# A layer norm turned by VectorE through exchanged reads, and two shifts in a hand-written order

## The chip, the cores and the metric

The kernel runs on one core of a Trainium2 chip. The metric is the device time of one launch in microseconds (us). Beside the matrix engine (PE) the core has VectorE (DVE), ScalarE (ACT) and GpSimd (POOL); SyncE (SP) issues nearly all DMAs, in order, and waits there for whatever a transfer needs.

## What is computed

One transformer block over 2,048 tokens of 1,024 channels: layer norm, linear attention with a learned feature map, output projection and residual; then layer norm, an MLP with relu over 3,584 channels, and residual. All in float32.

```python
def _layernorm(x, axis=-1, eps=1e-5):
    m = jnp.mean(x, axis=axis, keepdims=True)
    v = jnp.var(x, axis=axis, keepdims=True)
    return (x - m) / jnp.sqrt(v + eps)
...
        qkv = (lambda x, *d: x.transpose(*d))((x @ wqkv).reshape(B, S, 3, H, Dh), 2, 0, 3, 1, 4)
        q, k, v = qkv[0], qkv[1], qkv[2]
        pq = jnp.einsum("bhsd,hdf->bhsf", q, w_phi)
        pk = jnp.einsum("bhsd,hdf->bhsf", k, w_phi)
        phi_q = jnp.concatenate([_softmax(pq, axis=-1), _softmax(-pq, axis=-1)], axis=-1)
        phi_k = jnp.concatenate([_softmax(pk, axis=-1), _softmax(-pk, axis=-1)], axis=-1)
        kv = jnp.einsum("bhsf,bhsd->bhfd", phi_k, v)
        z  = jnp.einsum("bhsf->bhf", phi_k)
        num = jnp.einsum("bhqf,bhfd->bhqd", phi_q, kv)
        den = jnp.einsum("bhqf,bhf->bhq", phi_q, z)[..., None] + 1e-6
        o = num / den
        return (lambda x, *d: x.transpose(*d))(o, 0, 2, 1, 3).reshape(B, S, D) @ wo
...
    def _B_ref(x, w1, w2):
        h = jnp.einsum("bsd,df->bsf", x, w1)
        zero = jnp.zeros_like(h)
        h = jnp.maximum(h, zero)
        return jnp.einsum("bsf,fd->bsd", h, w2)
...
    x = A_x
    h = x + _A_ref(_layernorm(x, axis=-1), A_wqkv, A_w_phi, A_wo)
    h2 = h + _B_ref(_layernorm(h, axis=-1), B_w1, B_w2)
```

## The kernel before

**Products.** Every float32 product is made of three matmuls of a rounded type (L182, L183, L184): high half by high half, and the two mixed ones. So each weight tile of 128x512 comes in as `raw` (SP), is rounded to its high half by ACT (L125), and its low half, `raw` less the high one, is made by POOL or by DVE (L129). A ring of such weights lies ahead of PE; the engines work their queues in order. The activations are split in the same way.

**Stages and steps.** The program is written as one list of pieces of work. PE's part is counted in *steps*, one step being one set of three matmuls of 128x512; `when(step, f)` puts a piece of work of another engine, or a small product, beside that step. Eight steps make an item up to step 1,024, four after that. Steps 0 to 255 make keys and values of the first half of the tokens, 256 to 383 the queries of that half in two slabs of 64 steps (the second from 320), 384 to 767 the same for the second half, 768 to 1,023 the output projection with the rest of the attention beside it, then come the up products (from 1,024) and the down products of the MLP.

**Weight sums.** The MLP is done by Strassen and Winograd's scheme: seven products of half-size blocks instead of eight. Sums of weight blocks are made beforehand on POOL, 56 groups of them: `t_load` (SP, 512 KB, L352), four subtractions of 128x256 `t_sum` (POOL, L362) and `t_store` (SP, L365), at the steps of the table `sums_at` (L1090). The groups of the first half's query slabs use two buffers in turn. POOL's low halves (L129) stand in the same queue.

**The second layer norm.** The 16 token tiles are taken in pairs, `i` = 0 to 3 in each of the two halves ("near", b=0, done beside the output projection, and "late" or "far", b=1, beside the up products). `ln_pair` (L692) has stages: load of the two tiles from `hd` (SP), statistics (DVE, L221), scale (POOL, L230 to L232), the norm (ACT, L238, 128x1024 each), turning by PE in four groups of four transposes of 128x128 (`ln_turn`, L245; and L714) with copies out of PSUM (ACT, L247), the sums that the scheme needs of the tokens (DVE, L718 and L719; POOL, L724 and L725), and seven stores to `hs` (`ln_store`, L728). The table `LN2` (L1051) gives the steps of the stages: near pairs from 832 in distances of 40, far pairs from 1,084 in distances of 68. `h_load` (L738) later brings the turned tiles from `hs` into `hT` in 128x4x128 pieces; ACT (L750) and DVE (L754) split them for the up products. The first half's `hT` loads fall around step 1,024, when `hd` stores of the residual (L687) leave too.

**PSUM.** The up products go round four banks `mm` and two others (`ac`, `tp`); ACT (L777) or DVE (L780) drains a bank, and PE may write it again only then.

## Time and profile before

| | |
|---|---|
| time, median of 3 runs | 1894.32 us (1893.66 to 1894.36) |
| the profiled execution | 1895.65 us, its span 1893.9 us |
| granted PE clock, mean | 0.998 |
| PE | 1879.6 us busy, 11,640 matmuls |
| DVE, ACT, POOL | 1048.3, 740.3, 975.9 us busy |
| DMA | 432.17 MB, mean 228 GB/s |

The span runs from the first to the last instruction of the profiled execution. Busy time of PE is modelled, since its matmuls are pipelined: one is shown with 0.39 us while the next starts 0.23 us after it. So PE is best read from the starts of its matmuls, and a place where it stood still from the brackets of the timeline and the view of waits. The other engines may idle without cost as long as what they make is there in time.

### The profile page before, as it was taken

Reading aid. Unit: us, or ns where it says so; the run is one execution under the profiler, and the core shown is the slowest. Engines: PE = TensorE matmul, PEld = TensorE weight load, DVE = VectorE, ACT = ScalarE, POOL = GpSimd, SP = SyncE. Lnnn points to the kernel's source line nnn. Section 1 sums busy time; section 2 is a strip of 40 time slices with the busy share of each in tenths; the row PEclk is TensorE's granted clock in tenths of the full one; section 3 lists DMA queues with packets and bytes.
Section 4 is the critical chain, followed back from the end, with each engine's and each line's share of the span. In section 5 each row is a group of like instructions: output and inputs, shape, how many; then the busy total and the mean of one; then the engine's idle time right before and its main releaser. Section 6 shows DMA issues by size and latency. Waiting matters only on the chain.

```text
span 1893.9 us, 31847 instructions
## 1 busy us (share of the span) xinstructions
PE 1879.6 (99%) x11640; PEld 1541.0 (81%) x11640; DVE 1048.3 (55%) x1687; ACT 740.3 (39%) x1258; POOL 975.9 (52%) x959
## 2 busy tenths in 40 slices
PE   9999999999999999999999999999999999999999
PEld 7777778888788787888888888888888888888887
DVE  6787668677689776555544563334333433343333
ACT  5322235222233122255454554444444444444442
POOL 4887743888936988323333222222344444444443
PEclk9999999999999999999999999999999999999999
DMA  7888687566555676796877986666677677767775
GB/s 224 289 292 290 228 284 253 187 197 199 186 195 175 205 243 211 251 271 212 276 229 244 296 271 218 184 194 204 216 238 218 197 233 237 240 212 219 215 215 179
DMA packets 292365, 432.17 MB, mean 228 GB/s; under 512 B 24048, under 2 KB 150000, under 8 KB 292208
## 3 DMA queue, kind: packets, MB, share of 16 engines
q1 hardware_dynamic: 275312, 413.36, 68.8%
q10 hardware_dynamic: 16896, 16.78, 2.6%
q8 instruction: 91, 1.49, 0.3%
q14 instruction: 66, 0.54, 0.1%
HBM read 292.68 MB, written 137.36 MB: 227 GB/s over the span
## 4 chain that ended last, share of the span: by engine, by line
PE 87%; POOL 7%; DMA 3%; issue 1%; DVE 1%; SPq 0%; ACT 0%; POOLq 0%; ACTq 0%
PE mm L182 22%; PE mm L183 22%; PE mm L184 22%; PE ac L182 4%; PE ac L184 4%; PE ac L183 4%; PE tp L182 2%; PE tp L184 2%; PE tp L183 2%; POOL ez L575 2%; POOL b L362 1%; PE tp L245 1%; DMA b<-in_w_dram 1%; POOL w L129 1%; POOL qe L613 1%
## 5 line engine op out<-in xcount | busy, mean ns | idle before, releaser
L129 POOL TENSOR_TENSOR w<-raw,w 128x512 fp32r<-128x512 f32 x353 | 468.2, 1328 | 733.1 <-ACT w L125 696.4
L125 ACT ACTIVATE w<-raw 128x512 fp32r<-128x512 f32 x686 | 409.6, 628 | 506.1 <-PE mm L184 249.9
L129 DVE TENSOR_TENSOR w<-raw,w 128x512 fp32r<-128x512 f32 x333 | 272.1, 818 | 525.2 <-ACT w L125 522.0
L182 PE MATMUL mm<-w,xT 128*128 128x512 f32 x768 | 306.4, 399 | 0.0
L183 PE MATMUL mm<-w,xT 128*128 128x512 f32 x768 | 301.5, 393 | 4.1 <-POOL w L129 3.8
L184 PE MATMUL mm<-w,xT 128*128 128x512 f32 x768 | 300.4, 391 | 0.0
L182 PE MATMUL mm<-hT,w 128*128 128x512 f32 x672 | 262.6, 391 | 0.0
L183 PE MATMUL mm<-hT,w 128*128 128x512 f32 x672 | 261.7, 389 | 0.5 <-DVE hT L754 0.5
L184 PE MATMUL mm<-hT,w 128*128 128x512 f32 x672 | 261.6, 389 | 0.0
L183 PEld LDWEIGHTS mm<-w,xT 128*128 128x128 f32 x768 | 144.9, 189 | 34.6 <-POOL w L129 5.6
L362 POOL TENSOR_TENSOR b<-b 128x256 f32<-128x256 f32 x176 | 144.6, 822 | 54.9 <-DMA b<-in_w_dram 44.7
L182 PEld LDWEIGHTS mm<-w,xT 128*128 128x128 f32 x768 | 144.9, 189 | 34.2 <-issue 2.9
L184 PEld LDWEIGHTS mm<-w,xT 128*128 128x128 f32 x768 | 144.9, 189 | 30.9
L182 PE MATMUL mm<-w 128*128 128x512 f32 x392 | 152.5, 389 | 0.0
L183 PE MATMUL mm<-w 128*128 128x512 f32 x392 | 152.5, 389 | 0.0
L184 PE MATMUL mm<-w 128*128 128x512 f32 x392 | 152.5, 389 | 0.0
L183 PEld LDWEIGHTS mm<-hT,w 128*128 128x128 f32 x672 | 126.2, 188 | 26.8 <-DVE hT L754 1.1
L184 PEld LDWEIGHTS mm<-hT,w 128*128 128x128 f32 x672 | 126.2, 188 | 26.3
L182 PEld LDWEIGHTS mm<-hT,w 128*128 128x128 f32 x672 | 126.2, 188 | 25.8
L182 PEld LDWEIGHTS mm<-w 128*128 128x128 f32 x392 | 73.6, 188 | 15.3
L184 PEld LDWEIGHTS mm<-w 128*128 128x128 f32 x392 | 73.6, 188 | 15.3
L183 PEld LDWEIGHTS mm<-w 128*128 128x128 f32 x392 | 73.6, 188 | 15.2
(170 smaller groups left out, 3143.9 us busy)
## 6 DMA issues: line engine op xcount, KB each, us to landing
raw<-t SPq DMA_DIRECT2D x224, 256.0 KB, 3.8
raw<-ad SPq DMA_DIRECT2D x196, 256.0 KB, 3.0
raw<-in_w_dram SPq DMA_DIRECT2D x168, 256.0 KB, 3.0
ad<-c SPq DMA_DIRECT2D x112, 256.0 KB, 3.5
b<-in_w_dram SPq DMA_DIRECT2D x44, 512.0 KB, 5.7
t<-b SPq DMA_DIRECT2D x44, 512.0 KB, 5.0
ad<-s SPq DMA_DIRECT2D x84, 256.0 KB, 4.1
ed<-qe ACTq DMA_DIRECT2D x32, 512.0 KB, 4.3
```

What stands on the lines that cost most here:

```text
L125: nc.scalar.activation(w[:, 0, :], raw[1], AF.Copy)
L129: eng.tensor_tensor(out=w[:, 1, :], in0=raw[1], in1=w[:, 0, :].bitcast(F32), op=ALU.subtract)
L182: pe.matmul(ps, a_hi, b_hi, start=first, stop=False, skip_group_check=more)
L183: pe.matmul(ps, a_hi, b_lo, start=False, stop=False, skip_group_check=more)
L184: pe.matmul(ps, a_lo, b_hi, start=False, stop=last, skip_group_check=more)
L245: pe.transpose(pt[:, k, :], xn[:, (4 * j + k) * P:(4 * j + k + 1) * P], ident)
L362: pool.tensor_tensor(out=tsum[*u, *out], in0=tsum[*u, *a], in1=tsum[*u, *b], op=ALU.subtract)
L575: pool.tensor_tensor(out=ez, in0=e_q[u].rearrange("p (i h) s f -> p i (h s f)", i=4)[:, 2 * j:2 * j + 2, :], in1=zb[:, q, None, 256 * r:25 ...
L613: pool.tensor_tensor(out=e, in0=e, in1=sd[:, :, None].to_broadcast([P, 32, 32]), op=ALU.mult)
```

## The change

Three things are changed.

1. *Far pairs.* PE no longer turns them. The statistics of a far tile are taken by DVE from the residual sum while it is in the core (`far_stats`), POOL makes the scale as before, and `far_scale` writes mean and scale of each token, repeated four times, to a small DRAM tensor `scd` in pieces of 8 bytes. `far_pair` then loads the tile with *exchanged reads*: four DMAs of 32 partitions, so that a partition holds pieces of 128 channels of eight tokens; a reload of `scd` brings the scales into the same places. ACT norms it in eight pieces of 128x256 of one pair, in one stage; DVE turns each 32x32 block (`far_swap`), which with the exchange gives the turned tile. The sums follow as before. The stores and `h_load` for b=1 have other patterns: 512 pieces of 512 bytes a store; four DMAs of 32x4x256 for what were two of 128x4x128.
2. *Weight sums.* In the first half's query slabs six and four groups (9 and 12 steps apart) become four and five (10 apart), and one group moves to step 650.
3. *Near pairs 1 and 2.* The turn of pair 1 comes six steps later (its stores four); the loads of pair 2 come six steps later and the stages after that are drawn together.

```diff
+    scd = [dram.tile([2, 4 * P * 2], F32, name=f"scd{i}") for i in range(4)]
...
+    def far_stats(t, hf):
+        if hf == 0:
+            hst[t] = hp.tile([P, 2, 6], F32, name="hst", bufs=8)
+        v.bn_stats(out=hst[t][:, hf, :], in_=xh[t, hf])
+        if hf == 1:
+            xst["h", t] = mv = lnp.tile([P, 2], F32, name="mv", bufs=4)
+            v.bn_aggr(out=mv, in_=hst.pop(t))
+
+    def far_scale(t):
+        dst = scd[t % 4][t % HT // 4].rearrange("(a p s) -> p a s", a=4, s=2)
+        sp.dma_start(dst, xst.pop(("h", t))[:, None, :].to_broadcast([P, 4, 2]))
+
+    def far_swap(dst, src):
+        v.transpose(dst.rearrange("p (c t g) -> p g c t", c=8, g=4), src.rearrange("p (g c k) -> p g c k", g=4, c=8))
+
+    def far_pair(i, stage):
+
+        tiles = [HT + 4 * r + i for r in range(2)]
+        if stage < 2:
+            t = tiles[stage]
+            xnt["h", t] = x = lnp.tile([P, D], F32, name="xin")
+            for a in range(4):
+                sp.dma_start(x[32 * a:32 * (a + 1)].rearrange("t (g r f) -> t g r f", g=4, r=2),
+                             hd[t].rearrange("(t g) (r a f) -> a t g r f", g=4, r=2, a=4)[a])
+        elif stage == 2:
+            sp.dma_start(scx[:, 2 * i:2 * i + 2].rearrange("p r g s -> p r (g s)"),
+                         scd[i].rearrange("r (p f) -> p r f", f=8))
+        elif stage == 3:
+            for r, t in enumerate(tiles):
+                for g in range(4):
+                    x, sc = xnt["h", t][:, 256 * g:256 * (g + 1)], scx[:, 2 * i + r, g]
+                    act.activation(x, x, AF.Identity, bias=sc[:, 1:2], scale=sc[:, 0:1])
+        elif stage == 4:
+            x1, x2 = (xnt.pop(("h", t)) for t in tiles)
+            y2 = mp.tile([P, D], F32, name="y2", bufs=1)
+            sums[1, i] = x1, x2, y2
+            far_swap(y2, x2)
+        elif stage == 5:
+            s, y1, y2 = sums[1, i]
+            far_swap(y1, s)
...
+        sp.dma_start(hs[1, m][:, :, i], t.rearrange("p (k n) -> p k n", k=4))
...
+        if b == 0:
+            lo = hT[m][:, 1, :, cols].rearrange("p k (i n) -> p k i n", i=2)
+            for i in range(2):
+                sp.dma_start(f32(lo[:, :, i, :]), hs[b, m][:, 2 * g + i])
+            return
+        src = hs[b, m].rearrange("(a k) q i n -> q k a (i n)", a=4)
+        for q in range(4):
+            sp.dma_start(f32(hT[m][32 * q:32 * (q + 1), 1, :, cols]), src[q, :, :, cols])
...
+        if t >= HT:
+            when(added, far_stats, t, hf)
+            if hf == 1:
+                when(added + 4, ln_power, ("h", t))
+                when(added + 15, far_scale, t)
...
-    LN2 = ((0, 9, 12, 17, 24, 25, 26, 27, 29, 36), (0, 18, 26, 32, 40, 42, 44, 46, 50, 60))
+    NEAR = {1: (0, 9, 12, 17, 30, 31, 32, 33, 35, 40), 2: (6, 14, 17, 20, 24, 25, 26, 27, 29, 36)}
+    FAR = 0, 4, 8, 28, 34, 38, 42, 46, 54
...
-    sums_at = [30, 39, 47, 55] + [64 * i + k for i in (1, 2, 3, 4) for k in sixth] + [332, 344, 356, 368] + \
-        [64 * i + k for i in (6, 7, 8, 9) for k in sixth]
+    sums_at = [30, 39, 47, 55] + [64 * i + k for i in (1, 2, 3) for k in sixth] + \
+        [266, 276, 286, 296, 332, 342, 352, 362, 372] + [64 * i + k for i in (6, 7, 8, 9) for k in sixth] + [650]
```

What this does to the order of three queues follows; the changed kernel's lines are numbered a little higher (L362 becomes L363, L777 L843, L742 L804).

POOL, around the first half's query slabs (`b` are the weight sums, `w` the low halves of weights). Before:

```order
L362 TENSOR_TENSOR b<-b 128x256 x2
L129 TENSOR_TENSOR w<-raw,w 128x512
L362 TENSOR_TENSOR b<-b 128x256 x21
L129 TENSOR_TENSOR w<-raw,w 128x512
L362 TENSOR_TENSOR b<-b 128x256
L129 TENSOR_TENSOR w<-raw,w 128x512 x4
L362 TENSOR_TENSOR b<-b 128x256 x16
L129 TENSOR_TENSOR w<-raw,w 128x512 x4
```

Now:

```order
L363 TENSOR_TENSOR b<-b 128x256 x2
L129 TENSOR_TENSOR w<-raw,w 128x512
L363 TENSOR_TENSOR b<-b 128x256 x14
L129 TENSOR_TENSOR w<-raw,w 128x512 x5
L363 TENSOR_TENSOR b<-b 128x256 x20
L129 TENSOR_TENSOR w<-raw,w 128x512 x4
```

Before, 23 subtractions stand ahead of the first low half of the second slab and one more ahead of the next four; now 16 in all, and 20 instead of 16 ahead of the four after them.

ACT, in the up products where the third far pair is normed (`c<-mm` drains a PSUM bank, `w<-raw` is a high half). Before:

```order
L777 ACTIVATE c_10889<-mm 128x512
L125 ACTIVATE w<-raw 128x512
L777 ACTIVATE c_10926<-mm 128x512
L125 ACTIVATE w<-raw 128x512
L238 ACTIVATE xin<-xin,sc 128x1024 x2
L777 ACTIVATE c_10959<-mm 128x512
```

Now:

```order
L843 ACTIVATE c_10917<-mm 128x512
L125 ACTIVATE w<-raw 128x512
L769 ACTIVATE xin<-xin,scx 128x256 x8
L843 ACTIVATE c_10954<-mm 128x512
L125 ACTIVATE w<-raw 128x512
L843 ACTIVATE c_10985<-mm 128x512
```

The norms stood behind the second of these drains; the eight new ones stand ahead of it.

SP, around the start of the up products (`hd<-xh` stores the residual sum, `raw` loads weights, `hT<-hs` loads the turned tiles, `scd` are the new little writes). Now:

```order
L688 DMA hd_97<-xh 128x512
L748 DMA scd_114<-sc 128x4x2
L804 DMA hT_9207<-hs_2_103 128x4x128 x2
L338 DMA raw<-in_w_dram 128x512
L688 DMA hd_98<-xh 128x512
L338 DMA raw<-in_w_dram 128x512
L748 DMA scd_115<-sc 128x4x2
L688 DMA hd_99<-xh 128x512
L338 DMA raw<-t_2_316 128x512
L338 DMA raw<-t_3_317 128x512
L748 DMA scd_116<-sc 128x4x2
L804 DMA hT_9637<-hs_7_104 128x4x128 x2
```

The same rows stood there without the three `scd` writes; a fourth one follows two `hT` loads later, and four stand earlier, beside the stores of the first four far tiles.

More of the change, by code (lines that the diff above doesn't have):

```diff
@@ L687, in wo_store, with ln_pair @@
         sp.dma_start(hd[t][:, hf * 512:(hf + 1) * 512], xh.pop((t, hf)))
-    def ln_pair(b, i, stage):
-        keys = [("h", HT * b + 4 * r + i) for r in range(2)]
+    def ln_pair(i, stage):
+        keys = [("h", 4 * r + i) for r in range(2)]
         if stage == 0:
@@ L723, in ln_pair @@
-            s4 = (mp or hp).tile([P, 512], F32, name="s4l", bufs=1)
+            x1, s12 = xnt[keys[0]], sums[0, i]
+            s4 = hp.tile([P, 512], F32, name="s4l", bufs=1)
             pool.tensor_tensor(out=s12[:, 1, :], in0=s12[:, 0, :], in1=x1[:, 0:512], op=ALU.subtract)
             pool.tensor_tensor(out=s4, in0=x1[:, 512:], in1=s12[:, 1, :], op=ALU.subtract)
-            sums[b, i] = s12, s4
-    def ln_store(b, i, j):
-        x1, x2 = (xnt["h", HT * b + 4 * r + i] for r in range(2))
-        s12, s4 = sums[b, i]
+            sums[0, i] = s12, s4
@@ new lines @@
+    hst = {}
+    def far_scale(t):
[27 more added lines that the diff above has]
+            far_swap(y1, s)
+        elif stage == 6:
+            s, y1, y2 = sums[1, i]
+            v.tensor_add(s[:, 0:512], y2[:, 0:512], y2[:, 512:])
+            v.tensor_sub(y2[:, 0:512], y1[:, 0:512], y2[:, 0:512])
+        elif stage == 7:
+            s, y1, y2 = sums[1, i]
+            s4 = mp.tile([P, 512], F32, name="s4l", bufs=1)
+            pool.tensor_tensor(out=s[:, 512:], in0=s[:, 0:512], in1=y1[:, 0:512], op=ALU.subtract)
+            pool.tensor_tensor(out=s4, in0=y1[:, 512:], in1=s[:, 512:], op=ALU.subtract)
+            sums[1, i] = s, y1, y2, s4
@@ L1054 @@
     for i in range(4):
+        near, far = wo0 + 64 + 40 * i, up0 + 60 + 68 * i
+        ln2 = NEAR.get(i, (0, 9, 12, 17, 24, 25, 26, 27, 29, 36))
         for stage in range(9):
-            when(wo0 + 64 + 40 * i + LN2[0][stage], ln_pair, 0, i, stage)
-            when(up0 + 60 + 68 * i + LN2[1][stage], ln_pair, 1, i, stage)
+            when(near + ln2[stage], ln_pair, i, stage)
+        for stage in range(8):
+            when(far + FAR[stage], far_pair, i, stage)
         for j in range(7):
-            when(wo0 + 64 + 40 * i + LN2[0][9] + j // 2, ln_store, 0, i, j)
-            when(up0 + 60 + 68 * i + LN2[1][9] + j, ln_store, 1, i, j)
+            when(near + ln2[9] + j // 2, ln_store, i, j)
+            when(far + FAR[8] + j, far_store, i, j)
     assert wo_n[8, 0] + 10 < first_up
```

36 lines of the change are left out of this document (20 added, 16 removed).

## The prediction

> **What bounds the kernel now.** I read the page first, then the waits of the matrix engine, then the timeline at each of those waits (its rows: start, duration, engine, line, what is written and read; in brackets the idle time ahead and what ended it).
>
> ```profile
> span 1893.9 us, 31847 instructions
> PE 1879.6 (99%) x11640; PEld 1541.0 (81%) x11640; DVE 1048.3 (55%) x1687; ACT 740.3 (39%) x1258; POOL 975.9 (52%) x959
> ```
>
> PE is busy 99% of the span; no other engine passes 55%. So time can be won in two ways only: instructions taken off PE, and the few places where PE stands still or runs slowly. The profiled execution took 1895.65 us (its span and 1.75 around it); the median of the runs is 1894.32, 1.33 less. I sum against 1895.65 and take 1.33 off at the end.
>
> ```profile
> PE mm L183 <- POOL w L129: 3.8, 3, 3.2
> ...
> PE tp L245 <- DVE oT L651: 1.2, 1, 1.2
> ...
> PE mm L183 <- DVE hT L754: 0.5, 1, 0.5
> ```
>
> These are the waits that the change comes near: 3.8 us for low halves of weights from POOL, 1.2 for a transpose that DVE holds up, 0.5 for the operand of the up product.
>
> ```profile
> 263.72 0.39 PE L182 MATMUL mm<-w,xT 128*128 128x512 f32 x1
> ...
> 264.40 0.39 PE L182 MATMUL mm<-w,xT 128*128 128x512 f32 x1
> 267.99 0.79 PE L183 MATMUL mm<-w,xT 128*128 128x512 f32 x1 [3.20 <-POOL w L129]
> ...
> 269.91 0.79 PE L183 MATMUL mm<-w,xT 128*128 128x512 f32 x1 [0.27 <-POOL w L129]
> ...
> 274.34 0.53 PE L184 MATMUL mm<-w,xT 128*128 128x512 f32 x1
> ```
>
> From 263.72 to 264.40 are three starts, 0.227 us each: the pace of PE at full clock, and 0.68 us for a step of three products. The first wait costs more than its 3.20 us: from 269.91 to 274.34 ten starts take 4.43 us, 0.44 each, about half the pace. From 264.40 to 274.34 lie 14 starts, 3.17 us at the full pace; they take 9.94. **This place loses 6.77 us**: 3.47 of waiting, 3.30 of half clock.
>
> **Part 1, the weight sums.** What made POOL late:
>
> ```profile
> 239.49 3.19 POOL L362 TENSOR_TENSOR b<-b 128x256 f32<-128x256 f32 x4 [4.47 <-DMA b<-in_w_dram]
> ...
> 257.97 3.65 POOL L362 TENSOR_TENSOR b<-b 128x256 f32<-128x256 f32 x4 [3.01 <-DMA b<-in_w_dram]
> 264.37 2.34 POOL L362 TENSOR_TENSOR b<-b 128x256 f32<-128x256 f32 x3 [2.75 <-DMA b<-in_w_dram]
> 266.67 1.26 POOL L129 TENSOR_TENSOR w<-raw,w 128x512 fp32r<-128x512 f32 x1
> 267.89 0.73 POOL L362 TENSOR_TENSOR b<-b 128x256 f32<-128x256 f32 x1
> 268.58 3.74 POOL L129 TENSOR_TENSOR w<-raw,w 128x512 fp32r<-128x512 f32 x3
> ```
>
> From 239.49 to 264.37 are four groups, 6.22 us each. The table asks for one each 9 steps, 6.12 us, so the queue never catches up on its late beginning, and the sixth group stands ahead of the low halves that slab 1 needs from step 320 on; PE waits until 267.9 for the first of them. In the change slab 0 has four groups, asked for 10 steps (6.80 us) apart. The fourth group of the slab, which now is the last, ended already in the old order when POOL's idle time ahead of the fifth began, at 257.97 − 3.01 = 255.0, 11.7 us before the first late low half began at 266.67. With nothing behind it but low halves, POOL is ready long before PE arrives. Slab 1 gets five groups instead of four, 6.80 us apart, more than the 6.22 that a group takes. Its end is the place to look at:
>
> ```profile
> 290.44 3.20 POOL L362 TENSOR_TENSOR b<-b 128x256 f32<-128x256 f32 x4 [2.95 <-DMA b<-in_w_dram]
> 298.77 3.19 POOL L362 TENSOR_TENSOR b<-b 128x256 f32<-128x256 f32 x4 [5.13 <-DMA b<-in_w_dram]
> 304.09 3.20 POOL L362 TENSOR_TENSOR b<-b 128x256 f32<-128x256 f32 x4 [2.14 <-DMA b<-in_w_dram]
> 314.50 1.29 POOL L129 TENSOR_TENSOR w<-raw,w 128x512 fp32r<-128x512 f32 x1 [7.20 <-ACT w L125]
> ```
>
> The old last group was asked for at step 368 and ended at 307.3; the next low half then waited 7.20 us for ScalarE's high half. The new last one is asked for four steps (2.7 us) later, so some 4.5 of the 7.20 us remain as cover. The tenth group, now at step 650, falls where POOL has only low halves that wait for ScalarE. Value: −6.8 us. Ends: 0, if slab 1 slips and stalls as slab 0 did, and −6.8.
>
> **Part 2, the transposes.** Sixteen groups of four leave PE in the up products.
>
> ```profile
> 1028.58 0.39 PE L182 MATMUL ac<-hT,w 128*128 128x512 f32 x1
> ...
> 1029.26 0.60 PE L245 MATMUL tp<-ident,xin 128*128 128x128 f32 x4
> 1029.62 0.48 PE L182 MATMUL ac<-hT,w 128*128 128x512 f32 x1
> ...
> 1037.04 0.39 PE L184 MATMUL mm<-hT,w 128*128 128x512 f32 x1
> ```
>
> From 1028.58 to 1037.04 there are 29 intervals of the 0.227 pace around the four groups of one pair: 6.57 us without transposes, 8.46 with them. So a pair costs 1.89 us, 0.47 a group, and PE waits for nothing there: every nanosecond is on the path. Four pairs: **−7.5 us**.
>
> What comes in for it runs on engines and queues beside PE:
>
> ```profile
> 875.00:1040.00 165.00, 165.00 (x761) 136.66 (x760) 79.17 (x113) 83.44 (x136) 63.11 (x61) 1.00 0.73 235
> ...
> L619 DVE STREAM_TRANSPOSE qe<-qe 128x1024 f32<-128x1024 f32 x28 | 34.4, 1233 | 16.4 <-POOL qe L613 14.6 <-POOL qe L603 1.8
> ```
>
> In this stretch of the windows (columns: PE, its weight loads, DVE, ACT, POOL, clock, DMA share, GB/s) DVE works 79 of 165 us, POOL 63, DMA 0.73. Two DVE transposes of a pair are 2 × 1.23 us, in separate steps; a single one delays a drain of a product by at most 1.23 us, where a step of the up products, 12 matmuls, lasts 2.72. Value: nothing; without that cover 2.46 a pair, 9.9 in all. The reads in pieces of 512 bytes (2,048 a pair) and the stores in pieces of 512 instead of 2,048 bytes (3,584 a pair against 896) are bounded by the time of one packet:
>
> ```profile
> q1 hardware_dynamic: 275312, 413.36, 68.8%
> ```
>
> 68.8% of 16 engines over 1893.9 us, shared by 275,312 packets, are 76 ns a packet of 1,501 bytes, 20 bytes per ns. If a 512-byte piece takes its share by bytes (26 ns) nothing is added; if it takes a whole 76 ns, a pair costs 5,632/16 × 76 ns = 26.8 us instead of 8.6 (2.75 MB at 16 × 20 bytes per ns), 18 more, while the 27% that is idle over its 68 steps (46 us) is 12.5. The 5.5 us a pair beyond that would reach PE only after the loaded weights are used up. I take nothing and keep some of it above in the range. The pair's chain itself starts 60 steps into the up products and its last store leaves long before far products read it.
>
> The norms are another matter. ScalarE did two of 128x1024; now it does eight of 128x256 in one step, and for the third pair (i=2) that step stands one instruction earlier, ahead of a drain of PSUM (timeline of ACT, then of PE, then two groups of ACT with their mean):
>
> ```profile
> 972.54 0.64 ACT L125 ACTIVATE w<-raw 128x512 fp32r<-128x512 f32 x1 [1.60 <-issue]
> 973.08 0.58 ACT L777 ACTIVATE c<-mm 128x512 f32<-128x512 f32 x1
> ...
> 975.79 1.24 ACT L238 ACTIVATE xin<-xin,sc 128x1024 f32<-128x1024 f32 x1
> ...
> 975.01 0.39 PE L182 MATMUL mm<-hT,w 128*128 128x512 f32 x1
> ...
> L426 ACT ACTIVATE vt<-mm 128x256 f32<-128x256 f32 x64 | 24.5, 383 | 146.6 <-PE mm L184 146.6
> L523 ACT ACTIVATE qe<-qe 128x1024 f32<-128x1024 f32 x32 | 34.1, 1065 | 70.1 <-DVE qe L519 65.7 <-DMA ed<-qe 4.4
> ```
>
> The drain at 973.08 frees the bank that the product at 975.01 writes. An activation grows by (1065 − 383)/768 = 0.89 ns an element, so the 1.24 of a norm over 1024 is 0.56 over 256; in a row the next starts about 0.10 before the end of the last (972.54 + 0.64 against 973.08), so eight take 3.7 us. The drain then ends at 973.08 + 3.7 + 0.58 = 977.36, and PE waits **2.35 us**. Behind it on ScalarE stand the next high half and the next drain; weights are loaded and split some units ahead, so they add no wait of their own. Ends: with the 0.28 spacing that 0.383 gives when the overlap is taken off, 0.9 us; with 0.56 and no overlap, 3.1. I take 2.35, since the norm has two operands per partition, as L238 has.
>
> **Part 3, the second pair's turn.**
>
> ```profile
> 715.26 0.66 PE L245 MATMUL tp<-ident,xin 128*128 128x128 f32 x4 [1.20 <-DVE oT L651]
> ```
>
> The transposes of step 896 wait in PE's queue for DVE, which is behind with the turned attention output. Six steps later (4.1 us) it is done: −1.4 us with the slower matmul behind the wait. Loads of the third pair come 6 steps later on SP; the stores of the second one 4 steps. Ends: 0 to −1.4.
>
> **Part 4, the little writes.** The mean and scale of each far tile go to DRAM as 512 pieces of 8 bytes. Four of the eight writes stand on SP among the loads of hT (timeline of SP, a window, PE, and a row of the DMA issues):
>
> ```profile
> 820.68 0.32 SPq L687 DMA_DIRECT2D hd<-xh  x1
> ...
> 828.29 4.30 SPq L742 DMA_DIRECT2D hT<-hs  x4
> ...
> 797.00:845.00 48.00, 47.53 (x210) 38.91 (x209) 22.51 (x24) 23.51 (x34) 11.85 (x7) 1.00 0.98 299
> ...
> 837.98 0.50 PE L183 MATMUL mm<-hT,w 128*128 128x512 f32 x1 [0.47 <-DVE hT L754]
> ...
> wphi<-in_w_phi_dram SPq DMA_DIRECT2D x1, 128.0 KB, 2.5
> ```
>
> DMA is busy 0.98 of this window, and PE already waits 0.47 us for its end. Four writes put 128 packets on each of the 16 engines. From below: only bytes count, nothing, and a shift of order may even win the 0.47. From above: the wphi load, 1,024 pieces of 128 bytes, landed in 2.5 us, at most 39 ns a piece: 128 × 39 = 5.0 us. Since the 2.5 us hold the fixed latency of a load as well, I take a quarter of that bound, about 10 ns a piece, 1.2 us. The statistics that make them (16 of 0.68 us, DVE) are the old ones at an earlier place, with DVE busy 22.5 of these 48 us.
>
> **Sum.** 1895.65 − 6.8 − 7.5 − 1.4 + 2.35 + 1.2 = 1883.5 in the profile's frame, **1882.1 us** as a median.
>
> **The rivals.**
> 1. *No new stall*: the norms cost the low bound or the bank is free, the little writes nothing. 1882.1 − 3.5 = 1878.6. For it: the four writes are 16 KB; against it: the order of ScalarE is fixed and the drain plainly stands behind the norms.
> 2. *The sums still stall* (the change doesn't do what it says): the five groups of slab 1 slip as the six of slab 0 did, and the wait with its half clock stands at step 384 instead of 320. 1882.1 + 6.8 = 1888.9. For it: two buffers and one load after the other; in slab 1 two groups lay 8.3 us apart (290.44 to 298.77) though these were asked for 12 steps apart. Against: 6.80 > 6.22 and the 7.20 us of cover.
> 3. *Half clock behind the norms*: the wait at the third pair grows to what 267.99 shows. 3.2 + 3.3 instead of 2.35: 1886.2. It decides at some wait of at most that 3.20; where, no row shows. The Trainium skill, "TensorE: Matmul & The Clock Gate", section "HAM oscillation — how this bites in real kernels", asks for no idle gap of PE over about 3.4 us; the trace has the half clock behind 3.20 already.
> 4. *The little writes jam the DMA*, slower than before: an 8-byte piece that is fetched, merged and written back costs two packets of the mean 76 ns. 128 × 0.152 = 19.5 us at a place with no idle DMA, all of it before the operand that PE waits for: 1882.1 − 1.2 + 19.5 = 1900.4. It decides from (1894.32 − 1880.9)/128 = 105 ns a piece. Against it stands the wphi row with at most 39. The Trainium skill, "DMA: Bandwidth & Descriptors", section "Specifications", gives 512 bytes as the least for full rate and says that below it the engine reads, modifies and writes; no row of this case shows a write so small.
>
> **How the numbers follow.** The forecast 0.60, rival 1 0.14, rival 2 0.08, rival 3 0.08, rival 4 0.10. The likeliest's own range is 1879.5 to 1885. The range of 1876.5 to 1889.5 holds rivals 1 to 3 and leaves out rival 4; below it allows that another of the small waits goes too, above that DMA gives back part of those 5.5 us a pair. A difference of 0.2% is 3.8 us, what a measurement of this kernel can just tell. Faster: the forecast and rivals 1 to 3 less a little of rival 2, 0.89; within: 0.05, from rivals 2 and 4; slower: 0.06, the rest of rival 4.
>
> **What would show it.** Right: no wait for POOL's low halves near 262 and full clock there; the stretch that was 1028 to 1037 without a transpose, its products 0.227 apart; a single wait of 2 to 3 us for the drain behind eight norms, near 963 (975 less the 12 us won by then); for the operand of the up products, near 830, a wait of 1 to 2.5 us. Wrong: half clock anywhere after 20 us, a wait for a weight whose load is late, or a DMA share near 1 after 860. I would be plainly wrong if the far products waited for their hT, or if the first far tiles' writes took many us to land.

## The result and the profile after

The changed kernel takes 1903.04 us (median of 5 runs, 1897.97 to 1903.60) beside 1893.66 (1892.76 to 1894.36): a ratio of 1.0041, 95% interval 1.0026 to 1.0056. It was forecast 12 us faster and is 9 us slower. The profiled execution took 1903.04 us.

From the page of the changed kernel, its first lines and two rows of its DMA issues (KB each, median us from issue to landing):

```profile
span 1901.2 us, 31843 instructions
PE 1877.3 (99%) x11576; PEld 1538.4 (81%) x11576; DVE 1066.5 (56%) x1695; ACT 738.1 (39%) x1270; POOL 971.7 (51%) x959
...
scd<-sc SPq DMA_DIRECT2D x8, 4.0 KB, 8.7
scx<-scd SPq DMA_DIRECT2D x4, 8.0 KB, 5.7
```

PE has 64 matmuls fewer, and its busy time is 2.3 us less, but the span is 7.3 us longer. A write of 4 KB takes a median of 8.7 us to land; no row of loads of 256 KB or 512 KB before has more than 7.6. The waits of PE:

```profile
PE mm L182 <- ACT c L843: 4.9, 1, 4.9
PE tp L715 <- ACT xin L248: 4.1, 1, 4.1
PE mm L182 <- ACT hT L816: 3.1, 1, 3.1
PE mm L183 <- DVE hT L820: 3.0, 1, 3.0
```

The waits for POOL's low halves and for `oT` are gone from this view. Four others stand in their place, at three spots of PE's timeline:

```profile
781.21 1.12 PE L715 MATMUL tp<-ident,xin 128*128 128x128 f32 x4 [4.09 <-ACT xin L248]
781.98 0.78 PE L182 MATMUL mm<-w,oT 128*128 128x512 f32 x1
782.55 0.63 PE L183 MATMUL mm<-w,oT 128*128 128x512 f32 x1
782.98 0.63 PE L184 MATMUL mm<-w,oT 128*128 128x512 f32 x1
...
839.32 0.51 PE L182 MATMUL mm<-hT,w 128*128 128x512 f32 x1 [3.06 <-ACT hT L816]
842.84 0.79 PE L183 MATMUL mm<-hT,w 128*128 128x512 f32 x1 [3.01 <-DVE hT L820]
...
1116.96 0.80 PE L182 MATMUL mm<-hT,w 128*128 128x512 f32 x1 [4.90 <-ACT c L843]
```

Behind each spot products start 0.43 us apart for some 4 to 5 us, half the pace. Where the time came from and went is best read by comparing when each step begins in the two traces (us won or lost in a stretch of steps, worked out from the starts of the products; minus is won):

| steps, and what lies in them | changed kernel |
|---|---|
| 0 to 340: weight sums | −7.0 |
| 872 to 930: turn of near pair 1 | −1.4 |
| 930 to 1010: turn of near pair 3 (781 us) | +7.5 |
| 1010 to 1090: first up products (839 us) | +8.4 |
| 1090 to 1340: four far pairs | −7.5 |
| 1340 to 1500: first products of the far half (1117 us) | +7.5 |

So all three wins came as computed, 15.9 us together, and 23.4 us were lost at three places. The timeline of SP ahead of the first loss:

```profile
756.25 0.54 SPq L659 DMA_DIRECT2D xh<-in_x_dram  x1
756.84 0.63 SPq L748 DMA_DIRECT2D scd<-sc  x1
757.58 2.32 SPq L216 DMA_DIRECT2D xin<-hd  x2
759.99 0.38 SPq L688 DMA_DIRECT2D hd<-xh  x1
760.43 0.42 SPq L659 DMA_DIRECT2D xh<-in_x_dram  x1
760.94 0.84 SPq L748 DMA_DIRECT2D scd<-sc  x1
```

Two of the little writes leave here, among loads and stores. A window behind them (the last three columns are clock, DMA share and GB/s):

```profile
759.00:766.00 7.00, 7.00 (x151) 5.68 (x151) 4.62 (x11) 1.21 (x4) 1.32 (x4) 1.00 1.14 128
```

The DMA engines are busy all the time (1.14) and move 128 GB/s. The view of DMA issues from 755 to 775 gives the two `xin<-hd` behind the first little write 10.0 us to land, against a median of 5.6 before. Over 20 us, first the kernel before and then the changed one (the same 212 instructions of PE, which came 8.4 us later before):

```profile
763.00:783.00 20.00, 20.00 (x212) 16.36 (x211) 9.31 (x16) 4.43 (x8) 4.97 (x9) 1.00 1.02 317
```

```profile
755.00:775.00 20.00, 20.00 (x212) 16.21 (x210) 12.48 (x24) 3.45 (x6) 7.87 (x17) 1.00 1.09 206
```

So DMA moves 206 GB/s where it moved 317. SP's DMAs wait for earlier ones to land, and so the loads of `hT` leave 8.8 us later than in the old order:

```profile
765.59 8.35 SPq L338 DMA_DIRECT2D raw<-t  x4
774.06 1.62 SPq L804 DMA_DIRECT2D hT<-hs  x2
```

The norms of pair 3 come 3.0 and 6.6 us late, of which some 5 us were slack. ScalarE's next work is the split of `hT`. It waits for its load, and the copies of pair 3's transposes (L248), which the bracket of PE names, stand behind it:

```profile
779.62 1.06 ACT L816 ACTIVATE hT<-hT 128x1024 fp32r<-128x1024 f32 x1 [3.89 <-DMA hT<-hs]
780.58 1.07 ACT L248 ACTIVATE xin<-tp 128x512 f32<-128x512 f32 x2
```

The third loss has such a chain too: the drain for which PE waits stands on ScalarE behind the split of a turned tile of the far half, and that split waited 7.55 us for its load.

```profile
1115.36 1.06 ACT L816 ACTIVATE hT<-hT 128x1024 fp32r<-128x1024 f32 x1 [7.55 <-DMA hT<-hs]
1116.33 0.58 ACT L843 ACTIVATE c<-mm 128x512 f32<-128x512 f32 x1
```

### The profile page after: what moved, and what is told of

It is laid out like the page before. It is cut to its first block, busy times and chain, and to the rows that moved or that the text cites. A ratio compares the mean times of both kernels' runs of the same rounds, so it can differ in the third digit from the quotient of the medians.

```text
span 1901.2 us, 31843 instructions
## 1 busy us (share of the span) xinstructions
PE 1877.3 (99%) x11576; PEld 1538.4 (81%) x11576; DVE 1066.5 (56%) x1695; ACT 738.1 (39%) x1270; POOL 971.7 (51%) x959
## 4 chain that ended last, share of the span: by engine, by line
PE 91%; DMA 5%; POOL 2%; SPq 1%; issue 1%; DVE 1%; ACT 0%; ACTq 0%; POOLq 0%; DVEq 0%
PE mm L182 23%; PE mm L183 23%; PE mm L184 23%; PE ac L184 3%; PE ac L183 3%; PE ac L182 3%; DMA hT<-hs 3%; PE tp L184 2%; PE tp L183 2%; PE tp L182 2%; PE tp L246 1%; PE ac L465 1%; PE tp L634 1%; DMA hd<-xh 1%; POOL w L129 1%; PE ac L634 1%
## 5 line engine op out<-in xcount | busy, mean ns | idle before, releaser
L363 POOL TENSOR_TENSOR b<-b 128x256 f32<-128x256 f32 x176 | 145.1, 825 | 53.0 <-DMA b<-in_w_dram 38.3
```

The source lines that it names most:

```text
L363: pool.tensor_tensor(out=tsum[*u, *out], in0=tsum[*u, *a], in1=tsum[*u, *b], op=ALU.subtract)
```

## The experiments

The kernel before was timed again beside each, with medians of 1894.3 to 1895.3 us.

**The two changes of order alone** (the kernel before with the new `sums_at` and `NEAR`, far pairs as they were).

> The kernel before with the new steps of the weight sums and of the near pairs alone; far pairs are turned by the matrix engine as before. If these two parts do what the trace shows (6.95 and 1.4 us won), the time is 1885 to 1886.5. If the later weight sum at step 650 or the later loads of the third pair give something back, it is above 1888.

1886.87 us (1886.72 to 1887.95), ratio 0.9958 (0.9944 to 0.9973), 0.4 us above the range that was expected. The trace shows −6.9 and −1.3 us at the two places and nothing elsewhere. These parts are right, and nothing of them is given back.

**The little writes alone.**

```diff
+        if t >= HT and hf == 1:
+            when(8 * n + (11 if n < wo_first + 2 else 9) + 15, far_scale, t)
```

> The kernel before with the new steps of the weight sums and of the near pairs (1886.9 alone), and with the eight writes of 512 pieces of 8 bytes at the steps where the changed kernel has them, from a tile that nothing needs; far pairs as before. If the writes alone make the two waits, this kernel is 12 to 16 us slower than without them, 1899 to 1903. If it takes the rest of the far pairs' new order, it stays below 1890.

1899.09 us (1898.26 to 1901.18), 12.2 more than without the eight writes. The waits at the operand of the up products came back, 4.3 and 2.7 us long:

```profile
PE mm L182 <- ACT hT L756: 4.3, 1, 4.3
PE mm L183 <- DVE hT L760: 2.7, 1, 2.7
```

Steps 930 to 1010 lost 2.5 us and 1010 to 1090 lost 9.9. Eight transfers of 4 KB that nobody needs make the two losses; the second wholly and part of the first (7.5 in the changed kernel; why it is larger there was not tried, though the experiment with spread pieces below shows that the rest of the change makes none of it without such writes).

**What is it in such a write?** Six writes of other shapes, one at a time, in a stretch of the down products.

```diff
+    for k in range(6):
+        when(1900 + 100 * k, probe, k)
```

> The kernel before, with six writes of the scale tile added in the down products, 100 steps (68 us) apart, each to DRAM of its own; nothing else changes. In order: 512 pieces of 8 bytes side by side (as the changed kernel writes them); 128 pieces of 8 bytes side by side; 512 of 8 bytes, one each 64 bytes; 512 of 8 bytes, one each 512 bytes; 512 of 64 bytes side by side; 128 of 64 bytes side by side. If memory takes small neighbouring pieces one after another, some 11 ns each, the first holds up the transfers behind it for 5 to 6 us, the second for 1.4, and the third and fourth hardly at all, the last two hardly at all. If any small piece costs that, wherever it goes, the third and fourth hold up as much as the first. If a write costs only its place in SyncE's queue, all six look alike, under 1 us.

Windows of 4 us that begin 1.8 to 2.8 us after each issue (last two columns: DMA share, GB/s), in that order:

```profile
1420.00:1424.00 4.00, 4.00 (x19) 3.34 (x18) 1.39 (x2) 2.12 (x4) 1.29 (x1) 1.00 0.68 132
1487.00:1491.00 4.00, 4.00 (x19) 3.30 (x19) 0.69 (x1) 1.73 (x4) 1.79 (x2) 1.00 0.82 71
1556.00:1560.00 4.00, 4.00 (x19) 3.34 (x18) 1.39 (x2) 2.01 (x4) 1.64 (x2) 1.00 0.88 248
1623.00:1627.00 4.00, 4.00 (x19) 3.30 (x19) 3.77 (x5) 1.73 (x4) 1.80 (x2) 1.00 0.74 222
1691.00:1695.00 4.00, 4.00 (x19) 3.30 (x19) 0.69 (x1) 1.73 (x4) 1.79 (x2) 1.00 0.80 209
1759.00:1763.00 4.00, 4.00 (x19) 3.30 (x19) 0.69 (x1) 1.73 (x4) 1.79 (x2) 1.00 0.65 179
```

From issue to landing they took 6.5, 5.2, 4.0, 3.1, 3.5 and 2.6 us. The first two, pieces of 8 bytes side by side, bring the rest down to 132 and 71 GB/s. In the kernel before, which has no such writes, the same six windows moved 206, 189, 269, 188, 204 and 185 GB/s: so the same 512 pieces 64 or 512 bytes apart do little (248 for 269 and 222 for 188), and pieces of 64 bytes nothing that shows (209 for 204, 179 for 185). So it is neither the number nor the size alone but 8-byte pieces that lie together. That 128 pieces do about as much as 512 speaks against a fixed price per piece. In the records of single packets an 8-byte piece itself takes 9 ns everywhere; it is the other packets behind it that take long: single packets of 2 KB took up to 2.9 and 4.3 us behind the first two writes, at most 1.0 behind the others.

**A quarter of the pieces.** `scd` holds each scale once, and four loads repeat it.

```diff
-        sp.dma_start(dst, xst.pop(("h", t))[:, None, :].to_broadcast([P, 4, 2]))
+        sp.dma_start(dst, xst.pop(("h", t)))
```

> The changed kernel, but mean and scale of a far tile are written once (128 pieces of 8 bytes) instead of four times (512), and read back by four DMAs of 32 partitions. If the pieces hold up memory (about 11 ns each), a write costs 1.4 us instead of 5.5, the waits at 781 and 839 us with their half clock (7.1 and 8.4 us) go nearly wholly, and the time is 1886 to 1891. If only the place of a further DMA in SyncE's queue matters, their number is the same and the time stays at 1898 to 1904.

1899.60 us (1895.69 to 1905.28). The loss at 781 us fell from 7.5 to 2.9, that at 839 stayed (9.1). The time lies in the second range, but not by its reason: a mere place in SP's queue would not have made one loss smaller, and in the probe the spread pieces had a place too and cost little. The probe fits, in which the quarter jammed about as long as the whole.

**The same pieces, 64 bytes apart.**

```diff
-        dst = scd[t % 4][t % HT // 4].rearrange("(a p s) -> p a s", a=4, s=2)
+        dst = scd[t % 4][t % HT // 4].rearrange("(a p s) -> p a s", a=4, s=16)[:, :, 0:2]
```

> The changed kernel, with the pieces of 8 bytes written one each 64 bytes instead of side by side, and read back by two DMAs a pair instead of one. The number and size of the written pieces stay. If it is neighbouring pieces in one stretch of memory that hold up the transfers, the waits at 781 and 839 us (7.1 and 8.4 us with their half clock) become at most 2 us in all, and the time is 1887 to 1891, the wait at 1117 us being left. If any small write or any further DMA does it, the time stays at 1896 to 1904.

1889.80 us (1886.09 to 1895.14). The loss at 781 us is gone (0.0); at 839 it is 5.2 with one wait of 3.0; at 1117 it is 4.9. The time is as expected, though more of the second loss stayed than I had said. With the same pieces moved elsewhere it goes too ("Both", below), so pieces 64 bytes apart are not free at that place either.

**The same neighbouring pieces, later.** `far_scale` at steps 1068 to 1110, behind the loads of `hT`.

> The changed kernel with its writes of 512 neighbouring pieces of 8 bytes, but at steps 1068 to 1110, six apart, behind the loads of hT instead of among them. If the place decides, since transfers there have time to spare, the waits at 781 and 839 us (7.1 and 8.4 us) go and the time is 1887 to 1891, the wait at 1117 being left. If eight writes of 5 to 6 us each are too much anywhere, waits for weights appear between 848 and 880 us, and the time stays above 1893.

1894.78 us (1890.52 to 1897.56), above the first range and in the second (above 1893). The two losses are nearly gone (1.1 and 0.0), but the stretch of the far pairs, which won 7.5, now loses 1.1: the loss had moved with the writes. PE waits 4.2 us there, at 886.55, for a drain by VectorE and not for a weight as was said. (The traced run is the slowest of ten.) So the place alone does not mend it.

**Both** (the yardstick for what follows).

> The changed kernel with its pieces of 8 bytes 64 bytes apart and written at steps 1068 to 1110; the loads of the far half's turned tiles as in the change. It is the yardstick for the next two. The waits at 781 and 839 us are gone as in the last kernel but one; the wait near 1100 us for the drain (4.8 to 7 us with its half clock) is left: 1882 to 1886.

1886.32 us (1882.24 to 1888.24), ratio 0.9958 (0.9944 to 0.9972). The first two losses are 0.0 and −0.8, and one is left:

```profile
1099.32 0.79 PE L182 MATMUL mm<-hT,w 128*128 128x512 f32 x1 [4.02 <-ACT c L844]
1099.91 0.63 PE L183 MATMUL mm<-hT,w 128*128 128x512 f32 x1
```

It costs 6.8 us. ScalarE drains this bank behind the split of `hT`, and that split waits for its loads:

```profile
1097.72 1.06 ACT L817 ACTIVATE hT<-hT 128x1024 fp32r<-128x1024 f32 x1 [6.91 <-DMA hT<-hs]
1098.69 0.58 ACT L844 ACTIVATE c<-mm 128x512 f32<-128x512 f32 x1
```

**What makes these loads late?** First by themselves: 512 KB into a free tile, in five ways.

> The kernel before, with five loads of 512 KB into a free tile added in the down products, 120 steps (82 us) apart, from DRAM that is no longer written: four DMAs of 32 partitions with four pieces of 1 KB each (as the changed kernel loads the far half's turned tiles); two of 128 partitions with four pieces of 512 bytes (as before); four of 128 partitions with one piece of 1 KB; four of 32 partitions with one piece of 4 KB; one of 128 partitions with a piece of 4 KB. If writing into 32 partitions alone is what slows the pieces, the first shows about 80 ns a piece of 1 KB and the third about 50, and the fourth is slower than the fifth. If not, the first and the third agree.

Mean time of a packet, from the records of the packets of those moments:

```
4 x  32 partitions x 4 x 1 KB     88 ns
2 x 128 partitions x 4 x 512 B    27.5 ns
4 x 128 partitions x 1 x 1 KB     51 ns
4 x  32 partitions x 1 x 4 KB    233 ns  (median 228)
1 x 128 partitions x 1 x 4 KB    212 ns  (median 159)
```

A KB in one piece into 32 partitions alone takes 88 ns here where it takes 51 to 55 into all 128; with pieces of 4 KB the means differ little. The first load also ran in a fuller moment than the others (DMA share 1.06 against 0.75 to 0.87), so part of the 88 may be crowding. The packets of the kernels themselves, those that start from 1055 to 1125 us, have the same difference: 83 ns a KB into 32 partitions in the changed kernel and 74 in the yardstick, 30 for 512 bytes before, and 50 to 51 a KB into 128 partitions in two kernels further down, at a DMA share of 0.91. The far half's turned tiles are 7 MB, 7,168 pieces: (88 − 55) × 7168 / 16 = 14.8 us more of DMA time by the first figures, (83 − 60) × 7168 / 16 = 10.3 by the kernels' own. It falls where there is none to spare; windows 1060 to 1110 of the kernel before and of the changed one:

```profile
1060.00:1110.00 50.00, 50.00 (x222) 41.43 (x221) 27.87 (x32) 27.92 (x43) 14.61 (x9) 1.00 1.00 304
```

```profile
1060.00:1110.00 50.00, 50.00 (x222) 41.42 (x221) 27.66 (x32) 27.98 (x43) 13.94 (x9) 1.00 1.06 265
```

DMA is full in both, with 304 GB/s and with 265.

**Half as many loads of twice the size,** still into 32 partitions.

```diff
-        for q in range(4):
-            sp.dma_start(f32(hT[m][32 * q:32 * (q + 1), 1, :, cols]), src[q, :, :, cols])
+        for q in range(4 - 4 * g):
+            sp.dma_start(f32(hT[m][32 * q:32 * (q + 1), 1, :, :]), src[q])
```

> As the yardstick, but a far product's turned tiles come in four loads of 256 KB (32 partitions, four pieces of 2 KB) instead of eight of 128 KB, all at the step of the first four. The number in flight on SyncE's queue is eight at most in the traces (a DMA is issued when the one eight before it has landed), so half as many loads of twice the size move more at once. If the number makes them late, the wait near 1100 us goes and the time is 1878 to 1881. If writing into 32 partitions does, it stays, within 2 us of the yardstick.

1889.92 us (1887.72 to 1892.57), and the last loss grew to 9.7. So it is not the number of loads alone; half of them also stand three steps earlier in the order here, which was not tried apart.

**The splits later in ScalarE's order,** so that the drain goes first.

```diff
-            when(step + 13 + 4 * g, h_high, m, g)
-            when(step + 16 + 4 * g, h_low, m, g)
+            when(step + 17 + 4 * g, h_high, m, g)
+            when(step + 20 + 4 * g, h_low, m, g)
```

> The yardstick (1886.3), with the splits of the far half's turned tiles four steps later in the order, so that ScalarE drains the bank of m=6 before it waits for the tiles of m=3. If what PE waits for at step 1447 is only the order on ScalarE (the tiles are needed nine steps later), the wait of 4.0 us becomes one of at most 2.9 for the tiles themselves and the half clock behind it goes: 1880 to 1884. If the tiles are late in any order, the wait stays and so does the time.

> As the last, with the splits six steps later, the most that the order allows before the tiles are needed. 1880 to 1884 as well if the order on ScalarE is the cause, and the wait then stands at the tiles; above the yardstick if the splits now come too late for all seven products.

1890.12 (1885.21 to 1892.59) and 1888.23 us (1886.35 to 1894.20): no better. With four steps the drain no longer waits, and PE waits 11 us later for the tiles themselves (first PE; then what ended just before its wait of 2.48 us, the two halves of that tile's split, by ScalarE and by VectorE; the run shown is the fastest of eleven):

```profile
1107.56 0.49 PE L182 MATMUL mm<-hT,w 128*128 128x512 f32 x1 [0.61 <-ACT hT L817]
1110.54 0.50 PE L183 MATMUL mm<-hT,w 128*128 128x512 f32 x1 [2.48 <-DMA ad<-c]
1110.88 0.40 PE L184 MATMUL mm<-hT,w 128*128 128x512 f32 x1
...
1106.45 1.06 ACT L817 ACTIVATE hT<-hT 128x1024 fp32r<-128x1024 f32 x1 [1.51 <-DMA hT<-hs]
1109.27 1.21 DVE L821 TENSOR_TENSOR hT<-hT 128x1024 fp32r<-128x1024 f32 x1
```

The bracket at 1110.54 names a store, but the low half ended at 1110.48, right before it. The wait is under the 2.9 us that were expected; yet the half clock came all the same, from 1111.93 to 1114.92, and 5.3 us are still lost here (7.2 with six steps). The order decides which engine waits; the data are late in each of the three.

**The same loads into all 128 partitions,** one piece of 1 KB each (the spread pieces, and then all three mendings).

```diff
-        for q in range(4):
-            sp.dma_start(f32(hT[m][32 * q:32 * (q + 1), 1, :, cols]), src[q, :, :, cols])
+        for a in range(4):
+            sp.dma_start(f32(hT[m][:, 1, a, cols]), src[a, :, :, cols])
```

> The changed kernel with the pieces of 8 bytes 64 bytes apart (1889.8 alone), and with each of the four loads of the far half's turned tiles writing all 128 partitions with one piece of 1 KB instead of 32 partitions with four pieces. If the 32 partitions make the loads slow (in the probe 88 ns a piece beside 51), the pieces come to about 50 ns, the wait for the drain near 1105 us with its half clock (4.8 us) goes, and the time is 1884 to 1886; the wait at the up products' operand (5.2 us with its half clock) is left. If the number of loads makes them late, the wait and the 1889.8 stay.

> All three mendings: pieces 64 bytes apart, written at steps 1068 to 1110, loads of the far half's turned tiles into 128 partitions. If these are all that the change lost, what is left is what the forecast summed without its new waits: 1893.7 less 6.95, 1.4 and 7.5, that is 1878 to 1880. If a further wait was hidden behind the three, it is above 1882.

1934.99 (1932.73 to 1935.52) and 1933.01 us (1931.62 to 1933.94): 51 and 53 us are lost between steps 1340 and 1472. The pieces came to 50 ns as expected. But four such loads keep SP busy for long; its timeline in the second kernel, where four loads of 128 KB took 0.3 to 0.43 us each to issue in the yardstick:

```profile
1079.83 4.96 SPq L809 DMA_DIRECT2D hT<-hs  x4
1084.89 1.74 SPq L859 DMA_DIRECT2D ad<-c  x1
```

The first of four takes 0.5 us and the next three 1.0 to 1.4. The packets show a second thing: on the mean 3.7 of these 1 KB packets are in progress at once, ten in the yardstick, and the DMA share from 1055 to 1125 us is 0.48, as if such a load used a part of the engines only. Both expectations were wrong for a reason that neither had: each piece is fast, and yet the load is slow. Whether the slow issue or the few packets at once cost the 51 us, and what in these loads makes them so, was not tried. These two kernels therefore do not tell what loads into all 128 partitions are worth; the next ones do.

**The exchange in the stores:** four stores of 32 partitions for one, loads of 128 partitions as before; at first with stores as dense as in the change, then drawn out, then with the far pairs begun earlier.

> As the last, and the exchange between partitions is done by the stores of the far pairs (four of 32 partitions instead of one of 128) and no longer by the loads, which are two of 128 partitions with pieces of 1 KB, as many and as large as before the change. If it is the loads that make the drain at 1117 us late, that wait (7.25 us with its half clock) goes and the time is 1879 to 1883. If SyncE can't take the 84 further stores, waits for weights appear between 880 and 1080 us and it is above 1888.

> As the yardstick, but the exchange is done by the stores (four of 32 partitions for one), which are drawn out over 24 steps a pair instead of 6, and the loads are two of 128 partitions and 256 KB, as many as before the change. If it was only the crowding of the stores that cost time when they were four for one without being drawn out (1898.4), the time is 1878 to 1882, at or below the kernel with four loads of 256 KB. If reading or writing 32 partitions is slow wherever it stands, waits appear beside the stores and it is above the yardstick.

> The kernel whose stores do the exchange, drawn out (1888.8), with the far pairs beginning 16 steps earlier and 64 instead of 68 steps apart, so that the last pair's stores end 28 steps (19 us) earlier ahead of the loads that need them. If its wait at step 1400 (6.2 us) is loads that wait for these stores, it goes, and the time is 1880 to 1884. If SyncE's queue or the DMA engines cannot take the further stores anywhere, it stays above 1887.

1898.38 (1895.15 to 1900.64), 1888.78 (1886.82 to 1893.40) and 1887.06 us (1885.53 to 1888.78). (The first one's "as the last" is the kernel with spread pieces alone.) The third loss is 8.7 us in the first, which contradicts its expectation, 6.2 in the second and nothing in the last. So loads into 128 partitions alone do not take it away; they do when the stores ahead of them end early enough. But the stores are paid for elsewhere. At the first up products 3.2, 2.9 and 1.2 us are lost, and waits of 1.2 to 2.2 us come up among the far pairs, whose stretch wins 0.7, 2.5 and 0.0 us where it should win 7.5. 1880 to 1884 was expected of the last: the exchange has a price at either end.

**Half and half:** far pairs 0 and 1 as in the yardstick, 2 and 3 turned by PE and loaded as before.

```diff
-        if t >= HT:
+        if t >= HT and t % 4 < 2:
...
+            if i > 1:
+                when(far + (0, 18, 26, 32, 40, 42, 44, 46, 50)[stage], ln_pair, i, stage, 1)
```

> Far pairs 0 and 1 as in the yardstick (pieces of 8 bytes spread and late, exchanged reads, turned by VectorE), far pairs 2 and 3 turned by the matrix engine as before the change, their tiles loaded by DMAs of 128 partitions. Half the transposes come back (2 x 1.89 = 3.8 us), and half of the loads into 32 partitions go, some 7 us of DMA time between 1060 and 1110 us (7 MB at 88 instead of 55 ns a KB on 16 engines is 14.8 us for all of them). If it is the DMA time of these loads that makes PE wait near 1105 us, the wait is under 3 us without half clock behind it and the time 1882 to 1885. If it is not, the wait of 4 us with its half clock stays and the time is 1888 to 1891.

1884.43 us (1883.71 to 1891.81), ratio 0.9953 (0.9941 to 0.9965), within the expectation. In its traced run, the fastest, the wait of 4.0 us is one of 0.46, and the clock stays:

```profile
1099.47 0.50 PE L182 MATMUL mm<-hT,w 128*128 128x512 f32 x1 [0.46 <-ACT c L847]
1099.81 0.45 PE L183 MATMUL mm<-hT,w 128*128 128x512 f32 x1
```

Half of the 32-partition loads fit into the window there, all of them don't. One of its six runs took 1891.81; what waited in it is not known. This kernel also has half of the little writes, exchanged reads and stores, so that it is the loads rests on it together with the last kernel above, in which loads and stores differ from the yardstick and the far pairs begin earlier. Its median is the lowest of the kernels here, but its runs overlap with the yardstick's (1882.24 to 1888.24), and the intervals of the ratios with those of the two changes of order alone: it is not told apart from either.

## Why the prediction was wrong

*The sums* were forecast at −6.8 us and gave −7.0, with the five groups of slab 1 in time. That agreement is in part luck: the loss before differs from run to run. In the run of the five loads above, whose order here is the old one, it was 3.4 us smaller (a wait of 1.6 us, without half clock). *The turn of pair 1*: −1.4, and −1.4 measured. *The transposes*: −7.5, and −7.5 measured, 1.89 a pair four times. Reading a win from the starts of PE's matmuls around it held to 0.2 us in the trace it was read from.

*The norms* were forecast at +2.35 and cost nothing. The eight took 4.04 us (3.7 computed):

```profile
976.68 4.04 ACT L769 ACTIVATE xin<-xin,scx 128x256 f32<-128x256 f32 x8
980.63 0.58 ACT L843 ACTIVATE c<-mm 128x512 f32<-128x512 f32 x1
```

The drain came that late, and PE's products went on 0.227 us apart through it. So the step that failed is "the drain at 973.08 frees the bank that the product at 975.01 writes". That product waits for a semaphore of VectorE, which had drained its bank. By the order in which banks fall free, the bank drained at 973.08 is written again two items later, at 980.45; in the changed kernel at 984.06, 2.85 us after the end of the late drain at 981.21.

*The little writes* are the first main error: +1.2 us was taken; 12.2 us came by themselves, and 15.9 (7.5 and 8.4) at their two places in the changed kernel. The step was the upper bound of 39 ns a piece from the `wphi` row. Even the whole bound, 5.0 us for four writes, is less than what was measured. That row is a load: small pieces are read from DRAM. For a write of small neighbouring pieces no row of the trace before was near, so the bound was none. The packet records would not have shown it either, since the pieces keep 9 ns and the delay falls on the packets behind. The other four writes were put at nothing, without a reason; the loads of `hT` and pair 3 of the near half stood behind them.

Rival 4, at 0.10, came nearest: the little writes jam the DMA, and the kernel gets slower. Its time, 1900.4, was near by luck: it had 19.5 us at one place, from a price per piece, where 15.9 came at two places and another 7.5 from something else, and the probe shows a price per write, nearly the same for 128 pieces and 512. That a piece is fetched, merged and written back is not shown by any run. The Trainium skill, "DMA: Bandwidth & Descriptors", section "Specifications", which says that below 512 bytes the engine reads, modifies and writes, pointed the right way. The runs here show a high price for neighbours of 8 bytes only: pieces of 64 bytes, and of 8 bytes that lie 64 bytes apart, are also below 512, and in the probe they held up little (3.5 and 4.0 us to land, beside 6.5).

*The loads of the far half's turned tiles* are the second main error. They weren't in the sum at all, without a reason given: I costed the exchanged reads and the stores by packets, rightly at nothing, since the far pairs won their full 7.5 us, and wrote that a pair's last store "leaves long before far products read it". That is true and beside the point. The loads behind the stores cannot start earlier, since `hT` is free only when the near half's last product has read it; they fall into 50 us of full DMA (share 1.00 before), and each KB into 32 partitions took 83 ns there, where the old pieces took 60. Of a changed transfer I had priced two legs of three, and the third had no slack: +7.5 us. With half of these loads left away PE waited 0.46 us there instead of 4.0, and with loads into 128 partitions whose stores end early the loss is nothing.

*Rival 3* put half clock behind the norms. In the changed kernel it came at other places, behind waits of 3.0 us and more; in other runs behind shorter ones (last section).

Of the signs of being wrong that the prediction names, three came: half clock after 20 us, far products that wait for their `hT` (by way of ScalarE), and writes that take 8.7 us to land. A fourth, a DMA share near 1 after 860, could tell nothing: it stood in the trace before (1.00 from 1060 to 1110), behind the end of the window that the prediction read (0.73 from 875 to 1040). There the room for the loads could have been seen to be missing.

The changed kernel with writes spread and late is 1886.32: it has the win of 7.5 from the transposes and gives back 6.8 at the loads. That is why it ties with the two changes of order alone (1886.87).

## What to carry to other kernels

When work leaves the bound engine and turns into transfers, follow each tensor through every leg (write, store, load) and ask at each where it falls and how full DMA is there; a window with a share near 1.00 pays for every slower packet. Take no price for a write from a load: small pieces that lie together in DRAM should be tried on the chip before they are put ahead of anything that is waited for; 64 bytes apart they cost less, and still 5 us here where DMA was full. A win on the bound engine can be read to a few tenths of a microsecond when it is a count of products; what decides the sign is what the change puts into the queues.

## What the runs showed of the hardware

- A write of 128 or 512 pieces of 8 bytes side by side, 5.2 and 6.5 us to land, left 71 and 132 GB/s in a window of 4 us with DMA shares of 0.82 and 0.68, where the kernel before moved 189 and 206; with 512 pieces 64 bytes apart it was 248 where 269 had been.
- A packet of 1 KB into 32 partitions alone took 74 to 88 ns in these kernels, into all 128 it took 50 to 51; the first figures come from fuller moments, and with packets of 4 KB the means differ little (233 and 212).
- Half clock followed waits of PE much shorter than the 3.20 us of the trace before. After the first 25 us of these runs it followed every wait of 1.82 us or more but one (2.64 us, with loads into 128 partitions), and none of 1.73 us or less. The two nearest, in the second and third kernel with exchanged stores:

```profile
830.39 0.50 PE L183 MATMUL mm<-hT,w 128*128 128x512 f32 x1 [1.82 <-DVE hT L823]
```

```profile
831.05 0.50 PE L183 MATMUL mm<-hT,w 128*128 128x512 f32 x1 [1.73 <-DVE hT L823]
```

Behind the first, products start at half the pace from 831.76 to 834.75; behind the second they keep the full one.

One thing that looks like the chip is the program's: an SP DMA that waits is issued within 0.02 us of the landing of the one eight before it, because these DMAs take eight completion semaphores in turn.
